# A retention-then-gated-linear-unit kernel: the first two units interleaved by hand, zero products in their waits, and gated jobs of one unit for the first four units

## The chip, the core and the metric

The kernel runs on one core of a Trainium2 chip. The metric is device time in microseconds (us) of one execution; lower is better. A profile of one execution shows the engines TensorE (PE; its weight loads are PEld), VectorE (DVE), ScalarE (ACT), GpSimd (POOL) and the queues that issue DMAs (SPq, ACTq).

## What is computed

```
scores = (1/sqrt(D)) * q @ k^T                        # per batch b and head h
ret    = (scores * gamma_h ** (i - j) for i >= j) @ v # decayed causal mask, no softmax
x      = ret, heads side by side                      # (8, 576, 512)
gate   = sigmoid(sum over k of conv_w[k] * x[t-4+k])  # causal convolution, 5 taps, per channel
out    = (gate * (x @ w_val)) @ w_out                 # (8, 576, 512), float32
```

The inputs are float32: q, k, v of shape (8, 8, 576, 64), w_val and w_out of (512, 512), conv_w of (5, 512). The decay is split into a factor on v (`gin`) and a factor on the output (`gout`).

## The kernel before

**Units and jobs.** The sequence of each of 8 batches is cut into two units of 256 positions and a rest of 64; the rests of four batches make one more unit. So there are 18 units, 0 to 17. Attention is done unit by unit, the gated part job by job: jobs 0 and 1 hold one unit each (256 columns), the others two units (512 columns).

**One unit's attention.** Three loads of 512 KB (`load`, L93, on SP's queue); `cast` (L201) of k, q and v to bf16, on GpSimd except k and q of unit 0; `turn` (L217): 16 transposes on TensorE into the PSUM pool `ps_a`; `take_turn` (L228): two copies out, `kq`; `scores` (L234): 16 products of quarter size for each half `hf` of the heads, into `ps_s`; `masks` (L248): VectorE multiplies by the mask, `p`; `update` (L325): products of k and v into `ps_s` (unit 0: `ps_v`), a ScalarE copy `xf`, and GpSimd sums that make the carried states; `carried` (L264): products of q with the carried states; `values` (L294): products with v; `take_x` (L306): VectorE scales the result into `xg`.

**The gated part.** `conv` (L387): the convolution as products with diagonal blocks `dg` into `ps_a`, then a sigmoid on ScalarE (`gate`); `value` (L405): `xg` times `wvb` into `ps_v`; `gated` (L415): VectorE multiplies both (`z`); `project` (L421): `z` times `wob` into `ps_v`, and a ScalarE copy `ob`; `store` (L431), on SP's queue. A job's conv and value are cut in two pieces over two steps where it has two units. The weights are made bf16 by `prep_wv` (ScalarE, L185) and `prep_wo` (VectorE, L190); `prep_conv` (L173) builds `dg`.

**Order.** The program is written out under a manual schedule: every engine takes its instructions in the order of the Python calls, and semaphores carry the waits between engines. The loop at L459 runs steps n = 0 to 20. Step n does scores and masks of unit n, conv and value of the piece that `PH` names, the values of unit n, cast of unit n+2, update and turn of unit n+1, and the projections that `PJ` names. `ps_a`, `ps_s` and `ps_o` hold one tile each, `ps_v` two; so conv waits until `take_turn` has emptied `ps_a`, scores of the second half until masks of the first has emptied `ps_s`, and a projection until a `gated` has emptied a `ps_v`. Loads run four units ahead (`ldp`, 4 buffers). Ahead of the loop stand eight products of zeros (`warm`, L193).

Of the kernel before, what the change touches and what calls it, by code (L numbers as in the profile page):

```python
# [21 lines left out]
def kernel(  # L22
# [32 lines left out]
    gp = ctx.enter_context(tc.tile_pool(name="gp", bufs=1))  # L55
# [15 lines left out]
    jobs = [(u,) for u in range(NC2)] + [(u, u + 1) for u in range(NC2, NU, 2)]  # L71
# [4 lines left out]
    with tc.manual_schedule():  # L76
# [24 lines left out]
        wof = consts.tile([P, NP, DM], F32, name="wof")  # L101
        nc.sync.dma_start(out=wvf, in_=moe_w_val.rearrange("(o i) n -> i o n", i=P))
        load(1)
# [3 lines left out]
        for u in range(2, 5):  # L107
            load(u)


        ident = consts.tile([P, P], BF16, name="ident")
# [5 lines left out]
        zero = consts.tile([P, 512], BF16, name="zero")  # L117
        nc.vector.memset(zero, 0.0)
# [41 lines left out]
        nc.vector.tensor_copy(mask[hi], mask_h[hi])  # L160
        mask_t = consts.tile([P, 2, P], BF16, name="maskt")
        nc.vector.tensor_copy(mask_t, mask)
        for i in (0, 2):
            nc.vector.memset(mask_t[i * 32:i * 32 + 32].rearrange("p j (r a) -> p j r a", r=2)[:, :, :, 32:64], 0.0)
# [7 lines left out]

        def prep_conv():  # L173
# [4 lines left out]
            id2 = consts.tile([P, 64], F32, name="id2")  # L178
            nc.vector.tensor_tensor(id2, ident[:, 0:64], ident[:, 64:128], op=ALU.add)
            nc.vector.tensor_tensor(  # L180
# [12 lines left out]
        def warm(n):  # L193
            z = ps_v.tile([P, 512], F32, name="v")
            for i in range(n):
                nc.tensor.matmul(z, lhsT=zero[:, 0:P], rhs=zero, start=True, stop=True)
# [3 lines left out]

        def cast(u):  # L201
            kind, b, c = units[u]
            kb = bfp.tile([P, 2, H, D], BF16, name="kb")
            qb = bfp.tile([P, 2, H, D], BF16, name="qb")
            vb = bfp.tile([P, H, 2, D], BF16, name="vb")
            ke, qe = (nc.vector.tensor_copy, nc.scalar.copy) if u == 0 else (nc.gpsimd.tensor_copy,) * 2
            ke(kb.rearrange("p r h d -> p h r d"), loaded["k", u].rearrange("p h (r d) -> p h r d", r=2))  # L207
            qe(qb.rearrange("p r h d -> p h r d"), loaded["q", u].rearrange("p h (r d) -> p h r d", r=2))  # L208
            nc.gpsimd.tensor_tensor(vb.rearrange("p h r d -> p (h r) d"),  # L209
# [249 lines left out]
        for n in range(NPH):  # L459
# [30 lines left out]
            if n == 1:  # L490
                prep_wo()
# [45 lines left out]
```

## Time and profile before

| | us |
|---|---|
| median of 3 runs | 176.27 (175.94 to 179.36) |
| the profiled execution | 176.73 |
| its span, first to last instruction | 175.0 |
| busy: PE, PEld | 148.3, 92.9 |
| busy: DVE, POOL, ACT | 99.4, 97.9, 89.0 |
| DMA read and written | 30.42 MB, 9.44 MB |

Times in the profile count from the first instruction of the span. A timeline line gives the start, how long a group of like instructions lasted, the engine, the line of the kernel, the operation, what it writes and reads, its form and how many there are; in brackets stand the idle time of the engine ahead of it and what ended it. A group of matrix products overlaps its neighbours in the record, since the end of a product is modelled: of the 0.42 us of 16 score products, some 0.35 us pass before the next group can start.

### The profile page before, as it was taken

Reading aid. Unit: us, or ns where it says so; the run is one execution under the profiler, and the core shown is the slowest. Engines: PE = TensorE matmul, PEld = TensorE weight load, DVE = VectorE, ACT = ScalarE, POOL = GpSimd, SP = SyncE. Lnnn points to the kernel's source line nnn. Section 1 sums busy time; section 2 is a strip of 40 time slices with the busy share of each in tenths; the row PEclk is TensorE's granted clock in tenths of the full one; section 3 lists DMA queues with packets and bytes.
Section 4 is the critical chain, followed back from the end, with each engine's and each line's share of the span. In section 5 each row is a group of like instructions: output and inputs, shape, how many; then the busy total and the mean of one; then the engine's idle time right before and its main releaser. Section 6 shows DMA issues by size and latency. Waiting matters only on the chain.

```text
span 175.0 us, 6597 instructions
## 1 busy us (share of the span) xinstructions
PE 148.3 (85%) x2921; PEld 92.9 (53%) x2921; DVE 99.4 (57%) x148; ACT 89.0 (51%) x118; POOL 97.9 (56%) x117
## 2 busy tenths in 40 slices
PE   5460767689596699999999999999999999999970
PEld 2150656576454465656666565666656566643320
DVE  5642232975636583765858376585838568583200
ACT  3547172527280538466373836647383653723550
POOL 7247369996692859495675949567594900000000
PEclk9999999999999999999999999999999999999999
DMA  4999999999996999999796998888611203032325
GB/s 143 358 351 291 285 269 321 290 329 322 316 339 195 301 342 302 295 265 321 227 301 234 306 299 257 241 277 243 204 54 73 120 4 124 2 124 120 122 62 180
DMA packets 60298, 40.28 MB, mean 230 GB/s; under 512 B 1626, under 2 KB 56942, under 8 KB 60270
## 3 DMA queue, kind: packets, MB, share of 16 engines
q1 hardware_dynamic: 60240, 39.85, 75.6%
q8 instruction: 23, 0.38, 0.8%
q14 instruction: 5, 0.04, 0.1%
q10 hardware_dynamic: 30, 0.01, 0.0%
HBM read 30.42 MB, written 9.44 MB: 228 GB/s over the span
## 4 chain that ended last, share of the span: by engine, by line
PE 61%; ACT 2%; DVE 1%; issue 0%; ACTq 0%
PE v L426 16%; PE v L410 14%; PE a L394 10%; PE a L224 7%; PE s L241 5%; PE o L302 4%; PE o L279 2%; PE s L339 1%; ACT gate L398 1%; DVE z L417 1%; PE o L286 1%; ACT ob L429 0%; ACTq L398 0%
## 5 line engine op out<-in xcount | busy, mean ns | idle before, releaser
L251 DVE TENSOR_TENSOR p<-s,mask 128x1024 bf16<-128x1024 f32 x32 | 39.2, 1224 | 44.5 <-PE s L241 44.5
L229 ACT COPY kq<-a 128x1024 bf16<-128x1024 bf16 x35 | 33.8, 1015 | 15.5 <-PE a L224 11.8
L209 POOL TENSOR_TENSOR vb<-fvc,gin 128x1024 bf16<-128x1024 f32 x18 | 34.5, 1917 | 5.3 <-DMA fvc<-in_v_dram 5.1
L410 PE MATMUL v<-xg,wvb 128*128 128x512 bf16 (+1 forms) x160 | 34.3, 359 | 0.0
L426 PE MATMUL v<-wob,z 128*128 128x512 bf16 x144 | 34.0, 379 | 0.1
L347 ACT COPY xf<-s 128x512 f32<-128x512 f32 x15 | 8.8, 585 | 42.5 <-PE s L339 42.5
L417 DVE TENSOR_TENSOR z<-gate,v 128x512 bf16<-128x512 f32 x36 | 24.5, 683 | 6.4 <-ACT gate L398 6.3
L241 PE MATMUL s<-kq 64*64 64x128 bf16 x576 | 19.8, 230 | 7.6 <-ACT kq L229 3.4
L394 PE MATMUL a<-xg,dg 64*64 64x512 bf16 (+1 forms) x400 | 24.1, 372 | 2.0 <-DVE xg L313 1.2
L398 ACT ACTIVATE gate<-a 128x1024 f32<-128x1024 f32 x18 | 18.4, 1024 | 11.9 <-ACT ob L429 5.8
L429 ACT COPY ob<-v 128x512 f32<-128x512 f32 x36 | 20.0, 606 | 8.2 <-PE v L426 8.2
L313 DVE TENSOR_TENSOR xg<-o,gout 128x512 bf16<-128x512 f32 x32 | 22.1, 744 | 2.0 <-PE o L302 2.0
L241 PEld LDWEIGHTS <-kq 64*64 64x64 bf16 x576 | 14.5, 109 | 15.2 <-issue 9.6
L410 PEld LDWEIGHTS <-wvb 128*128 128x128 bf16 x160 | 14.1, 97 | 14.0 <-issue 0.8
L426 PEld LDWEIGHTS <-z 128*128 128x128 bf16 x144 | 13.4, 98 | 14.1 <-issue 0.7
L207 POOL CAST kb<-fkc 128x1024 bf16<-128x1024 f32 x17 | 17.6, 1038 | 5.7 <-DMA fkc<-in_k_dram 5.7
L208 POOL CAST qb<-fqc 128x1024 bf16<-128x1024 f32 x17 | 17.7, 1040 | 0.9 <-DMA fqc<-in_q_dram 0.9
L394 PEld LDWEIGHTS <-dg 64*64 64x64 bf16 x400 | 13.6, 111 | 7.7 <-issue 2.8
L279 PE MATMUL o<-kq,s 64*64 64x128 bf16 x192 | 12.3, 220 | 5.8 <-POOL s L352 4.5
L224 PE MATMUL a<-ident,kb 128*128 128x128 bf16 x144 | 14.8, 230 | 2.5 <-DVE kb L207 2.5
L361 POOL TENSOR_TENSOR mid<-run,xf 128x256 f32<-128x256 f32 x8 | 5.8, 729 | 17.0 <-ACT xf L347 17.0
L279 PEld LDWEIGHTS <-s 64*64 64x64 bf16 x192 | 10.1, 108 | 8.8 <-POOL s L352 4.7
(60 smaller groups left out, 130.6 us busy)
## 6 DMA issues: line engine op xcount, KB each, us to landing
fkc<-in_k_dram SPq DMA_DIRECT2D x16, 512.0 KB, 6.0
fqc<-in_q_dram SPq DMA_DIRECT2D x16, 512.0 KB, 6.6
fvc<-in_v_dram SPq DMA_DIRECT2D x16, 512.0 KB, 7.3
out_dram<-ob SPq DMA_DIRECT2D x16, 512.0 KB, 3.4
wvf<-in_moe_w_val_dram SPq DMA_DIRECT2D x1, 1024.0 KB, 7.6
wof<-in_moe_w_out_dram SPq DMA_DIRECT2D x4, 256.0 KB, 7.2
fkc<-in_k_dram SPq DMA_DIRECT2D x8, 128.0 KB, 4.4
fqc<-in_q_dram SPq DMA_DIRECT2D x8, 128.0 KB, 4.4
```

The costliest lines, as they stand in the source:

```text
L209: nc.gpsimd.tensor_tensor(vb.rearrange("p h r d -> p (h r) d"), loaded["v", u].rearrange("p h (r d) -> p (h r) d", r=2), gin[:, c].rearran ...
L224: nc.tensor.transpose(ps[:, hf, i, prl, r, :], bf[u][i][:, r, h:h + 2, :].rearrange("p h d -> p (h d)"), ident)
L229: (eng or nc.scalar.copy)(kqt[u][hf].rearrange("p i l r c a -> p (i l r c a)"), tps[u][:, hf].rearrange("p i l r a -> p (i l r a)"))
L241: nc.tensor.matmul(s[half[c], par, prl, r, :], lhsT=t[half[par], 0, prl, r, c, :], rhs=t[half[par], 1, prl, :, c, :], start=True, stop=Tru ...
L251: nc.vector.tensor_tensor(p.rearrange("p e l r a -> p (e l) (r a)"), sps[u, hf].rearrange("p e l r a -> p (e l) (r a)"), m.rearrange("p r ...
L279: nc.tensor.matmul(o[rows, c, pr, :], lhsT=st[rows, pr, :], rhs=t[rows, 1, pr % 2, :, c, :], start=first(u, c, par), stop=False, skip_grou ...
L313: nc.vector.tensor_tensor(x[:, b, :, PAD + i0:PAD + i0 + P].rearrange("p o (a r) -> p o r a", r=2), o[:, c].rearrange("p o (r a) -> p o r ...
L394: nc.tensor.matmul(g[cols, bank, si, :], lhsT=dg[rows, blk, kk, :], rhs=xs(j, rows, blk, kk), start=(si == 0 and kk == 0), stop=(si == len ...
L398: nc.scalar.activation(t, g, AF.Sigmoid)
L410: nc.tensor.matmul(vp[:, si, :], lhsT=wvb[:, o, 2 * e + s, :], rhs=xs(j, slice(0, P), o, PAD), start=(si == 0 and o == 0), stop=(si == len ...
L417: nc.vector.tensor_tensor(zsb[j][:, 2 * e + ss[0]:2 * e + ss[-1] + 1, :], gsb[j, i][:, e], vps[j, i, e], op=ALU.mult)
L426: nc.tensor.matmul(o, lhsT=z[:, r, :], rhs=wob[:, jj, :], start=(jj == 0), stop=(jj == NP - 1))
```

## The change

It changes the first part of the program and the cut of the jobs:

- The loads of unit 1 are issued ahead of w_val instead of behind it; loads up to unit 6 are issued before the loop.
- The zero tile is VectorE's first instruction. `warm(8)` is replaced by `fill(n)`, called six times, 26 products in all, between other parts of the first two units.
- `dg` is built on GpSimd instead of VectorE. The casts of unit 0 are cut: k on VectorE, q half on ScalarE and half on VectorE; q of unit 1 is on ScalarE.
- `prep_mask_t` (for the tail units) is moved behind unit 1's attention.
- The attention of units 0 and 1 is written out by hand. The second scores of unit 0 go to `ps_a`; unit 0's values are done chunk by chunk; the second transposes of unit 1 are ahead of the rest of unit 0; `update` of units 0 and 1 uses `ps_v`; a dummy sigmoid loads ScalarE's table early.
- Then come, still ahead of the loop, conv, value and gated of jobs 0 and 1, with the w_out cast (`prep_wo`) on VectorE between the two jobs, projection of unit 0, turn of unit 2, projection of unit 1, update of unit 2, and the cast of unit 3.
- Jobs 0 to 3 have one unit each; from unit 4 on, jobs have two. The loop starts at n = 2. In step 2 there is no piece, in step 3 all of job 2, in steps 4 and 5 the two pieces of job 3; from step 6 on, the pieces fall on the same steps and the same units as before, and the projections too, except that units 2 and 3 are projected in steps 3 and 5 instead of 5 and 6.
- In a step, `carried(n, 1)` stands ahead of the second scores instead of among them, and `carried(n, 0)` between the two values calls instead of ahead of the second scores.
- The gate tile has two buffers instead of one, and in the last two steps the second half of a projection is copied by VectorE.

```diff
-    gp = ctx.enter_context(tc.tile_pool(name="gp", bufs=1))
+    gp = ctx.enter_context(tc.tile_pool(name="gp", bufs=2))
...
-    jobs = [(u,) for u in range(NC2)] + [(u, u + 1) for u in range(NC2, NU, 2)]
+    jobs = [(u,) for u in range(2 * NC2)] + [(u, u + 1) for u in range(2 * NC2, NU, 2)]
...
+        load(1)
         nc.sync.dma_start(out=wvf, in_=moe_w_val.rearrange("(o i) n -> i o n", i=P))
-        load(1)
...
-        for u in range(2, 5):
+        for u in range(2, 7):
...
+        zero = consts.tile([P, 512], BF16, name="zero")
+        nc.vector.memset(zero, 0.0)
...
-        zero = consts.tile([P, 512], BF16, name="zero")
-        nc.vector.memset(zero, 0.0)
...
-        nc.vector.tensor_copy(mask[hi], mask_h[hi])
         mask_t = consts.tile([P, 2, P], BF16, name="maskt")
-        nc.vector.tensor_copy(mask_t, mask)
-        for i in (0, 2):
-            nc.vector.memset(mask_t[i * 32:i * 32 + 32].rearrange("p j (r a) -> p j r a", r=2)[:, :, :, 32:64], 0.0)
+        def prep_mask():
+            nc.vector.tensor_copy(mask[hi], mask_h[hi])
+        def prep_mask_t():
+            nc.vector.tensor_copy(mask_t, mask)
+            for i in (0, 2):
+                nc.vector.memset(mask_t[i * 32:i * 32 + 32].rearrange("p j (r a) -> p j r a", r=2)[:, :, :, 32:64], 0.0)
...
+        id2 = consts.tile([P, 64], F32, name="id2")
+        nc.gpsimd.tensor_tensor(id2, ident[:, 0:64], ident[:, 64:128], op=ALU.add)
         def prep_conv():
             cps = ps_a.tile([P, KC * NP], F32, name="a")
             nc.tensor.transpose(cps, cwn, identf[0:KC * NP, 0:KC * NP])
             cw = consts.tile([P, KC * NP], F32, name="cw")
             nc.vector.tensor_copy(cw, cps)
-            id2 = consts.tile([P, 64], F32, name="id2")
-            nc.vector.tensor_tensor(id2, ident[:, 0:64], ident[:, 64:128], op=ALU.add)
-            nc.vector.tensor_tensor(
+            nc.gpsimd.tensor_tensor(
                 dg.rearrange("p o k j -> p k o j"),
                 cw.rearrange("p (k o) -> p k o", o=NP).unsqueeze(3).to_broadcast([P, KC, NP, 64]),
                 id2.unsqueeze(1).unsqueeze(1).to_broadcast([P, KC, NP, 64]), op=ALU.mult)
...
-        def warm(n):
+        def fill(n):
...
+        def cast1(u, n, eng=None, hs=slice(0, H)):
+            kind, b, c = units[u]
+            if (n, u) not in bf:
+                bf[n, u] = bfp.tile([P, H, 2, D] if n == "v" else [P, 2, H, D], BF16, name=f"{n}b")
+            t, src = bf[n, u], loaded[n, u]
+            if n == "v":
+                nc.gpsimd.tensor_tensor(t.rearrange("p h r d -> p (h r) d"), src.rearrange("p h (r d) -> p (h r) d", r=2),
+                                        gin[:, c].rearrange("p h r -> p (h r)").unsqueeze(2).to_broadcast([P, 2 * H, D]),
+                                        op=ALU.mult)
+            else:
+                (eng or nc.gpsimd.tensor_copy)(t[:, :, hs, :].rearrange("p r h d -> p h r d"),
+                                               src[:, hs].rearrange("p h (r d) -> p h r d", r=2))
         def cast(u):
-            kind, b, c = units[u]
-            kb = bfp.tile([P, 2, H, D], BF16, name="kb")
-            qb = bfp.tile([P, 2, H, D], BF16, name="qb")
-            vb = bfp.tile([P, H, 2, D], BF16, name="vb")
-            ke, qe = (nc.vector.tensor_copy, nc.scalar.copy) if u == 0 else (nc.gpsimd.tensor_copy,) * 2
-            ke(kb.rearrange("p r h d -> p h r d"), loaded["k", u].rearrange("p h (r d) -> p h r d", r=2))
-            qe(qb.rearrange("p r h d -> p h r d"), loaded["q", u].rearrange("p h (r d) -> p h r d", r=2))
-            nc.gpsimd.tensor_tensor(vb.rearrange("p h r d -> p (h r) d"),
-                                    loaded["v", u].rearrange("p h (r d) -> p (h r) d", r=2),
-                                    gin[:, c].rearrange("p h r -> p (h r)").unsqueeze(2).to_broadcast([P, 2 * H, D]),
-                                    op=ALU.mult)
-            bf[u] = (kb, qb, vb)
+            for n in "kqv":
+                cast1(u, n)
...
+        def turn1(u, hf, i):
+            if u not in tps:
+                tps[u] = ps_a.tile([P, 2, 2, 2, 2, P], BF16, name="a")
+                kqt[u] = [tp_sb.tile([P, 2, 2, 2, 2, 64], BF16, name=f"kq{x}") for x in range(2)]
+            for prl in range(2):
+                for r in range(2):
+                    h = 2 * (2 * hf + prl)
+                    nc.tensor.transpose(tps[u][:, hf, i, prl, r, :],
+                                        bf["kq"[i], u][:, r, h:h + 2, :].rearrange("p h d -> p (h d)"), ident)
+        def turn(u):
+            for hf in range(2):
+                for i in range(2):
+                    turn1(u, hf, i)
...
-        def scores(u, hf, between=None):
-            s = ps_s.tile([P, 2, 2, 2, P], F32, name="s")
+        def scores(u, hf, pool=None):
+            s = (pool or ps_s).tile([P, 2, 2, 2, P], F32, name="a" if pool else "s")
...
-                    if between and prl == 0 and r == 0:
-                        between()
...
-        def fence(u, rows):
-            t = consts.tile([P, 1], F32, name="fence", bufs=2)
-            nc.vector.tensor_copy(t[rows], ops[u][rows, 1, 0, 0:1])
-        def values(u, hf):
-            vb = bf[u][2]
+        def fence(u):
+            t = consts.tile([P, 1], F32, name="fence")
+            nc.vector.tensor_copy(t[lo], ops[u][lo, 1, 0, 0:1])
+        def values(u, hf, chunks=(0, 1)):
+            vb = bf["v", u]
+            if u not in ops:
+                ops[u] = ps_o.tile([P, 2, NP, P], F32, name="o")
             o = ops[u]
             p = pt[u, hf]
             for prl in range(2):
                 pr = 2 * hf + prl
                 for r in range(2):
                     for (c, par) in QUAD:
-                        nc.tensor.matmul(o[half[par], c, pr, :], lhsT=vb[half[c], 2 * pr + par, r, :],
-                                         rhs=p[half[c], par, prl, r, :], start=first(u, c, par),
-                                         stop=(r == 1), skip_group_check=True)
-        def take_x(u):
+                        if c in chunks:
+                            nc.tensor.matmul(o[half[par], c, pr, :], lhsT=vb[half[c], 2 * pr + par, r, :],
+                                             rhs=p[half[c], par, prl, r, :], start=first(u, c, par),
+                                             stop=(r == 1), skip_group_check=True)
...
+        def take_x(u, chunks=(0, 1)):
...
+            for c in chunks:
...
-        def update(u):
+        def update(u, early=False):
...
-            if u == 0:
+            kb, vb = bf["k", u], bf["v", u]
...
-        def sets(j, i):
-            return (0, 1) if len(jobs[j]) == 1 else (i,)
-        def conv(j, i):
-            n, ss = width(j), sets(j, i)
-            g = ps_a.tile([P, 2, len(ss), n], F32, name="a")
+        gps = {}
+        def conv(j, ss, take=True):
+            n = width(j)
+            gt = ps_a.tile([P, 2, 512], F32, name="a")
+            g = gt[:, :, 0:len(ss) * n].rearrange("p e (s t) -> p e s t", s=len(ss))
...
+            gps[j, ss] = g
+            if take:
+                take_gate(j, ss)
+        def take_gate(j, ss):
+            n = width(j)
             t = gp.tile([P, 2, len(ss), n], F32, name="gate")
-            nc.scalar.activation(t, g, AF.Sigmoid)
-            gsb[j, i] = t
-            if i == 0:
+            nc.scalar.activation(t, gps[j, ss], AF.Sigmoid)
+            gsb[j, ss] = t
+            if j not in zsb:
...
-        PH = {1: [(0, 0)], 2: [(1, 0)], 3: []}
-        PJ = {2: [(0, 0)], 3: [(1, 0)]}
-        for j in range(NC2, len(jobs)):
-            n = 2 * j
-            PH[n], PH[n + 1] = [(j, 0)], [(j, 1)]
-            PJ[n + 1] = [(j, 0)]
-            PJ[n + 2] = [(j, 1)]
-        NPH = 2 * len(jobs) + 1
-        warm(8)
+        vcopy, scopy = nc.vector.tensor_copy, nc.scalar.copy
+        h0, h1 = slice(0, 4), slice(4, 8)
+        def value_all(j, ss, e):
+            value(j, ss, e)
+            gated(j, ss, e)
+        def proj(j, m, eng=None):
+            for r in range(2):
+                project(j, m, r, eng if r else None)
+            store(jobs[j][m])
+        fill(10)
+        prep_gout((0, 1))
+        cast1(0, "k", vcopy)
+        prep_mask()
         prep_conv()
-        prep_gout((0, 1))
-        cast(0)
-        turn(0, ((0, 0), (1, 0), (0, 1), (1, 1)))
-        take_turn(0, 0, nc.vector.tensor_copy)
+        turn1(0, 0, 0)
+        turn1(0, 1, 0)
+        fill(4)
+        cast1(0, "q", scopy, h0)
+        cast1(0, "q", vcopy, h1)
+        prep_gout((2,))
+        turn1(0, 0, 1)
+        turn1(0, 1, 1)
+        take_turn(0, 0, vcopy)
         take_turn(0, 1)
-        for n in range(NPH):
+        prep_gout((3,))
+        fill(2)
+        cast1(0, "v")
+        scores(0, 0)
+        masks(0, 0)
+        scores(0, 1, ps_a)
+        masks(0, 1)
+        dummy = consts.tile([P, 1], F32, name="dummy")
+        nc.scalar.activation(dummy, lsc, AF.Sigmoid)
+        cast1(1, "k")
+        fill(5)
+        update(0, True)
+        cast1(1, "q", scopy)
+        values(0, 0, (0,))
+        values(0, 1, (0,))
+        take_x(0, (0,))
+        turn1(1, 0, 0)
+        turn1(1, 1, 0)
+        carried(0, 1)
+        fence(0)
+        turn1(1, 0, 1)
+        turn1(1, 1, 1)
+        cast1(1, "v")
+        values(0, 0, (1,))
+        carried(0, 0)
+        values(0, 1, (1,))
+        take_turn(1, 0, vcopy)
+        take_turn(1, 1)
+        take_x(0, (1,))
+        fill(3)
+        scores(1, 0)
+        masks(1, 0)
+        conv(0, (0, 1), False)
+        update(1, True)
+        take_gate(0, (0, 1))
+        carried(1, 1)
+        scores(1, 1)
+        masks(1, 1)
+        prep_wv()
+        fill(2)
+        values(1, 1)
+        carried(1, 0)
+        values(1, 0)
+        take_x(1)
+        prep_mask_t()
+        cast(2)
+        value_all(0, (0, 1), 0)
+        conv(1, (0, 1))
+        value_all(0, (0, 1), 1)
+        prep_wo()
+        value_all(1, (0, 1), 0)
+        value_all(1, (0, 1), 1)
+        proj(0, 0)
+        turn(2)
+        take_turn(2, 0)
+        take_turn(2, 1)
+        proj(1, 0)
+        update(2)
+        cast(3)
+        PH = {3: (2, (0, 1)), 4: (3, (0,)), 5: (3, (1,))}
+        PJ = {3: [(2, 0)], 5: [(3, 0)]}
+        for j in range(2 * NC2, len(jobs)):
+            n = 2 * j - 2
+            PH[n], PH[n + 1] = (j, (0,)), (j, (1,))
+            PJ.setdefault(n + 1, []).append((j, 0))
+            PJ.setdefault(n + 2, []).append((j, 1))
+        NPH = 2 * len(jobs) - 1
+        for n in range(2, NPH):
             att = n < NU
             if n + 5 < NU:
                 load(n + 5)
-            piece = PH.get(n, [])
+            piece = PH.get(n)
             if att:
                 scores(n, 0)
                 masks(n, 0)
-            if n == 0:
-                cast(1)
-                update(0)
-                prep_gout((2, 3))
-            for (j, i) in piece:
-                conv(j, i)
+            if piece:
+                conv(*piece)
             if att:
-                if n == 0:
-                    scores(n, 1)
-                    masks(n, 1)
-                    carried(n, 0)
-                    fence(0, hi)
-                    carried(n, 1)
-                    fence(0, lo)
-                    prep_wv()
-                else:
-                    carried(n, 0)
-                    scores(n, 1, lambda: carried(n, 1))
-                    masks(n, 1)
-            for (j, i) in piece:
+                carried(n, 1)
+                scores(n, 1)
+                masks(n, 1)
+            if piece:
                 for e in range(2):
-                    value(j, i, e)
-                    gated(j, i, e)
-            if n == 1:
-                prep_wo()
+                    value_all(*piece, e)
             if att:
                 values(n, 1)
+                carried(n, 0)
                 values(n, 0)
                 take_x(n)
             if n + 2 < NU:
...
                 take_turn(n + 1, 0)
                 take_turn(n + 1, 1)
             for (j, m) in PJ.get(n, []):
-                project(j, m, 0)
-                project(j, m, 1)
-                store(jobs[j][m])
+                proj(j, m, vcopy if n >= NPH - 2 else None)
```

## The prediction

> **What bounds the kernel now.** I read the page's slices first, then the busy time by stage, then the chain that ended last, and last the timeline of the first 75 us.
>
> ```profile
> PE   5460767689596699999999999999999999999970
> ...
> DMA  4999999999996999999796998888611203032325
> ```
>
> ```profile
> 20.00:25.00 5.00, 3.69 (x95) 3.21 (x88) 1.54 (x3) 2.50 (x3) 2.08 (x2) 1.00 0.98 280
> ...
> 50.00:60.00 10.00, 6.91 (x169) 4.51 (x172) 5.58 (x7) 5.00 (x7) 5.93 (x7) 1.00 0.89 260
> ...
> 70.00:100.00 30.00, 30.00 (x638) 18.72 (x636) 19.64 (x24) 17.43 (x24) 21.16 (x25) 1.00 0.93 276
> ```
>
> ```profile
> 75.24 1.22 PE a L394 x20
> ...
> 77.20 1.83 PE v L410 x8
> 79.03 0.57 PE o L302 x32
> 79.60 0.25 PE s L339 x32
> 79.86 1.00 PE a L224 x16
> 80.86 1.73 PE v L426 x8
> 82.58 0.35 PE s L241 x16
> 82.93 1.22 PE a L394 x20
> ```
>
> A slice is 4.4 us, and the columns after the window's length are PE, PEld, DVE, ACT and POOL. From 60 us on TensorE never stops, and the chain repeats one step each 7.69 us (82.93 - 75.24), all of it TensorE's own work: conv 1.2, value 1.8, projection 1.7, attention 3.0. So what the change can win lies ahead of 60 us, where waits between engines rule, and it is kept only as far as the steady part starts earlier.
>
> ```profile
> 1.90 3.60 PE L196 MATMUL v<-zero 128*128 128x512 bf16 x8 [1.90 <-DVE tok L123]
> ...
> 25.06 2.35 PE L394 MATMUL a<-xg,dg 64*64 64x256 bf16 x40 [0.27 <-ACT kq L229]
> ...
> 31.33 1.90 POOL L209 TENSOR_TENSOR vb<-fvc,gin 128x1024 bf16<-128x1024 f32 x1 [0.22 <-PE v L410]
> ...
> 31.87 2.45 DVE L191 CAST wob<-wof 128x2048 bf16<-128x2048 f32 x1
> ...
> 33.09 1.93 ACT L229 COPY kq<-a 128x1024 bf16<-128x1024 bf16 x2 [0.31 <-PE a L224]
> ...
> 34.15 0.42 PE L241 MATMUL s<-kq 64*64 64x128 bf16 x16 [1.10 <-ACT kq L229]
> ...
> 35.76 1.29 PE L394 MATMUL a<-xg,dg 64*64 64x256 bf16 x40 [1.19 <-DVE xg L313]
> ...
> 42.86 0.42 PE L241 MATMUL s<-kq 64*64 64x128 bf16 x16
> 43.05 1.09 ACT L429 COPY ob<-v 128x512 f32<-128x512 f32 x2
> ...
> 53.86 0.30 PE L241 MATMUL s<-kq 64*64 64x128 bf16 x7 [1.44 <-issue]
> ...
> 75.18 1.27 PE L394 MATMUL a<-xg,dg 64*64 64x512 bf16 x20
> ```
>
> The scores of units 2 and 3 start at 34.15 and 42.86. The 75.18 row is the conv of step 7: up to it both kernels have done the same units, pieces and projections, and behind it they do the same work. I therefore follow the new order to that conv and compare.
>
> The same 40 products took 2.35 us at 25 us and 1.29 at 36, so TensorE ran at half speed early, though the granted clock reads 1.00 in each window. Each zero product took some 0.43 us.
>
> **The change, step by step.** I take every engine's new order, in turn, with the durations of the rows.
>
> Start, up to unit 0's scores. The zero tile is ready at about 1.1 (VectorE waited until 1.40 for the identity), ten zero products at 0.43 end at 5.5. k of unit 0 is cast at once on its landing (0.69, done 5.5, before at 8.2). The small transpose and copy for `dg` free `ps_a` at 6.1. The q cast waits for its load (6.14) and ends at 6.7. With TensorE at full speed: k transposes 0.6, four zeros 0.86, q transposes 0.6, to 8.1; VectorE's copy 0.69, then ScalarE's 1.01, to 9.9; first mask 9.35 to 10.55, second to 11.8. At half speed these products take 1.03 + 1.7 + 1.06, and all is 1.8 later.
>
> `dg` on GpSimd is not in the trace. GpSimd's rows give 1.9 ns per column (vb) to 2.8 ns (L361, 0.73 us for 256), so 1280 columns cost 2.4 to 3.6; I take 2.4, the row with a like broadcast. It ends at 8.5, vb of unit 0 at 10.5; the longer end would add up to 0.5. It saves VectorE 1.7 us ahead of the k cast.
>
> Units 0 and 1. The load of unit 1 passes w_val (1024 KB, about 3 us), so its waits at 12.37, 13.84 and 15.73 become about 9.3, 10.8 and 12.5; w_val lands near 15.7, and unit 2 stays at 22.4 to 25.4, the bytes ahead of it being the same. After ScalarE's gout 0.8 and table load 1.28 (to 12.15), xf 0.65 to 12.8 and q of unit 1 1.04 to 13.9. GpSimd: s, run, s 1.5 to 14.0, vb 1.9 to 15.95. TensorE transposes q of unit 1 to 14.5, finishes unit 0's values at 15.0; copies of kq to 15.2 and 16.2; scores of unit 1 at 15.6 (before 24.15), conv of job 0 16.25 to 17.45 (before 25.06). Then xf, gate, w_val cast 0.65 + 1.02 + 2.16, to 21.7; the state of unit 1 at 19.35, its second scores to 20.05, mask to 21.3, values with carried 0.9, take_x 1.38 to 23.6. Here the new kernel is 8 us ahead of the old one.
>
> Where the lead goes. VectorE's queue then holds: the tail mask (0.5, to 24.1), gated, gated, the w_out cast, gated, gated. Conv of job 1 must wait for take_x and ends at 24.85, the second value product at 25.75, its gated at 26.5, the w_out cast 2.45 at 28.95, the next gated at 29.65. Only that frees a `ps_v` for the first projection, 29.7 to 31.5, and behind it in TensorE's queue stand the transposes of unit 2, though its casts are done at 27.3. They end at 32.5. ScalarE then has kq 1.93, ob 1.09, xf 0.58, to 36.15, and the scores of unit 2 wait for that xf to empty `ps_s`: 36.2, against 34.15 before. GpSimd idles from 27.3 to 36.15, since the cast of unit 3 is queued behind the state of unit 2 that needs this xf: 1.5 + 3.9, to 41.55. Update 0.35, transposes 1.0, kq 1.0: scores of unit 3 at 43.95, against 42.86.
>
> Steps 3 to 6. In step 3 GpSimd's next cast (3.9) and the state (1.15) hold the carried products to 46.6; then scores 0.65, value 1.85, values 0.85, update and turn 1.25, projection 1.75: unit 4 at 53.0. Step 4 has no projection, and its two masks are 1.22 each with little between: values at 56.3 to 57.05, turn to 58.3, kq 1.0: unit 5 at 59.35. Step 5: the second kq to 60.3, conv, carried and scores to 61.45, mask 1.23 to 62.7, values 0.8, turn 1.25, projection 1.75: unit 6 at 66.5 (before 67.15). Step 6 without projection is 5.95 and then shows kq's 1.93: conv of step 7 at 74.4, against 75.18. The sum is -0.7 us.
>
> Cut of jobs 2 and 3: 40 convs of 256 columns took 1.1 to 1.3, 20 of 512 took 1.2; 16 value products 1.85 against 1.83. I take 0. Order in a step: 8 carried products alone took 0.2 to 0.3, among the scores some 0.2, so 0 to 0.1 for each of 12 steps; and the second scores wait for the mask anyway (68.85 to 68.90). I take 0, and keep +1.2 for the range. The VectorE copy at the end replaces 0.58 on ScalarE; nearest are 0.69 and 0.75: -0.1 to +0.2, I take 0. The second gate buffer takes no wait away, since the last gated is long done. SP's queue: the loads of unit 7 now stand behind two stores, as DMA writes of 512 KB each some 3 us together; unit 7 landed by 54 and is cast after 57, so this is hidden; without the cover it would cost those 3 us.
>
> The stall of 1.44 us at 53.86, which no engine's wait explains, is in the old span alone in my sum; a like one is worth 0 to 1.9. I add 0.4, since most of the new waits would hide it.
>
> [...]
>
> Total: 176.73 - 0.7 + 0.4 = 176.4 by the profiled run; the median of the runs is 0.46 lower. I say 176.0.
>
> **Rivals.** (1) The lead of 8 us at job 0 is largely kept. For it: TensorE has only some 27.5 us of work between 36 and 74 (five attentions of 3.0, three convs with values of 3.0, two projections of 1.7), so 10 us of slack is there to win, and the queue waits are summed by hand. Against: in-order queues, the w_out cast ahead of gated, the GpSimd chain. Without the 2.45 cast in the way, and with half of unit 3's wait (2 us) gone: 171.5.
>
> (2) TensorE stays at half speed through unit 1, as it did up to 25 us before. Then the fills themselves cost: 1.8 at the first scores, 1.1 more for the five zeros and 0.6 for three, 1.1 in the conv, and 1.0 in transposes and scores: 5.6 later at conv of job 0, all of which the chain behind carries on: 181.5. If speed comes with the five zeros, only 2.0 is lost: 178. It decides if half speed lasts past some 14 us. For it: eight zeros did not suffice before. Against: ten, and more right behind.
>
> (3) The order does what it says and nothing is won: this is my forecast, lead given back.
>
> **How the numbers follow.** A difference under 2% (3.5 us) can hardly be told here from none. Forecast with full speed early 0.45 and with speed by the five zeros 0.18, both within 2%; rival 1 0.2; rival 2 0.17. So faster 0.2, same 0.63, slower 0.17. The likeliest case alone runs from 174.5 (no stall, -1 from shorter waits) to 178.5 (carried order +1.2, stall 1.9). The range takes in most of both rivals: 171.5 to 181.0.
>
> **What would show it.** Right: scores of unit 1 near 16, conv of job 0 near 17 at 1.2 us, the w_out cast right ahead of the first projection, scores of unit 2 near 36, GpSimd idle for 8 us before them, conv of step 7 near 74. Wrong: scores of unit 2 before 33 (rival 1), or conv of job 0 at 2.3 us and later than 20 (rival 2), or a steady step off 7.69 us.

## The result, and the profile after

The changed kernel takes 185.22 us (median of 4 runs, 183.07 to 186.86), against 176.47 (175.94 to 179.36) for the kernel before, run beside it: 1.0423 times as long, interval 1.0319 to 1.0528. The prediction said 176.0 and a range to 181.0. The profiled run took 184.44, with a span of 182.5. Some executions of a kernel last 1.5% or more beyond its shortest one, so ratios, intervals and differences between kernels below go by the mean of the others (183.76 for the change, 176.29 for the kernel before).

The slices of the changed kernel's page, 4.56 us each:

```profile
PE   7878369854699869969999999999999999999980
PEclk9999957997569999987999999999999999999997
DMA  4999999999996699599388989879822023022216
```

TensorE starts at once, as planned, and from about 84 us on it never stops (in the kernel before, from 60 on). New is the second line: the granted clock dips three times, at about 23, 43 and 81 us. The share by stage of the changed kernel (length, then PE, PEld, DVE, ACT, POOL busy, granted clock, DMA share, GB/s):

```profile
20.00:30.00 10.00, 6.88 (x114) 4.67 (x115) 4.73 (x7) 3.11 (x6) 5.72 (x6) 0.66 1.05 310
40.00:50.00 10.00, 5.77 (x139) 4.67 (x132) 4.44 (x5) 2.51 (x3) 9.87 (x11) 0.67 1.05 332
80.00:90.00 10.00, 9.50 (x180) 5.83 (x181) 5.13 (x6) 4.25 (x5) 6.37 (x8) 0.83 0.78 225
90.00:120.00 30.00, 30.00 (x638) 18.91 (x627) 20.46 (x24) 17.27 (x25) 21.11 (x24) 1.00 0.87 256
```

The trace's clock records place the spells: full from 5.84, half for 6.83 us from 22.91, half for 10.24 from 43.39, half for 3.41 from 80.94, full from 84.35 to 179.93. That is 20.5 us at half speed behind the first release. The last window is the steady part, and it is like the one before the change.

The chain of the changed kernel that ended last, at the first convs (start, length):

```profile
80.92 2.35 PE a L408 x19
...
90.20 1.27 PE a L408 x20
...
91.95 1.83 PE v L430 x8
...
97.90 1.27 PE a L408 x20
```

The convs are those of steps 7, 8 and 9. The steady step is 97.90 - 90.20 = 7.70 us, as before, and the conv of step 8 stands at 90.20 where it stood at 82.93: 7.27 of the profiled runs' 7.71 us are lost ahead of it. The timeline of the changed kernel up to there (start, length, engine, line, in brackets the idle time ahead and what ended it):

```profile
15.84 0.42 PE L254 MATMUL s<-kq 64*64 64x128 bf16 x16
...
16.20 1.29 PE L408 MATMUL a<-xg,dg 64*64 64x256 bf16 x40
...
19.03 0.41 PE L353 MATMUL v<-vb,kb 64*64 64x64 bf16 x26 [1.48 <-issue]
...
25.95 1.32 DVE L166 COPY maskt<-mask 128x256 bf16<-128x256 bf16 x1
...
27.68 2.27 PE L408 MATMUL a<-xg,dg 64*64 64x256 bf16 x40
...
31.57 1.22 DVE L196 CAST wob<-wof 128x2048 bf16<-128x2048 f32 x1
...
39.70 0.42 PE L254 MATMUL s<-kq 64*64 64x128 bf16 x16 [1.38 <-ACT xf L361]
39.72 0.40 POOL L366 CAST s<-xf 128x256 bf16<-128x256 f32 x1 [12.53 <-ACT xf L361]
...
48.71 0.64 PE L254 MATMUL s<-kq 64*64 64x128 bf16 x16 [1.10 <-ACT kq L242]
49.62 2.35 PE L408 MATMUL a<-xg,dg 64*64 64x256 bf16 x40 [0.27 <-ACT kq L242]
...
80.92 2.35 PE L408 MATMUL a<-xg,dg 64*64 64x512 bf16 x20 [0.49 <-ACT kq L242]
```

Unit 1's scores (15.84) and the conv of job 0 (16.20) stand where they were predicted (15.6, 16.25). From there the kernel falls behind its forecast. The 40 products of a conv take 1.29 us at 16.20, but 2.27 and 2.35 at 27.68 and 49.62: these two lie in the half-speed spells.

### The profile page after: what moved, and what is told of

Same layout as the page of the kernel before. It is cut to its first block, busy times and chain, and to the rows that moved or that the text cites. A ratio compares the mean times of both kernels' runs of the same rounds, so it can differ in the third digit from the quotient of the medians.

```text
span 182.5 us, 6766 instructions
## 1 busy us (share of the span) xinstructions
PE 158.3 (87%) x2995; PEld 99.5 (55%) x2995; DVE 101.7 (56%) x151; ACT 87.7 (48%) x119; POOL 98.5 (54%) x118
## 4 chain that ended last, share of the span: by engine, by line
PE 51%; DVE 1%; ACT 1%; issue 0%; ACTq 0%
PE v L445 14%; PE v L430 11%; PE a L408 10%; PE a L233 5%; PE o L317 4%; PE s L254 4%; PE o L290 2%; PE s L353 1%; ACT gate L418 1%; DVE z L436 1%; PE o L297 1%; DVE ob L448 0%; ACTq L418 0%
## 5 line engine op out<-in xcount | busy, mean ns | idle before, releaser
L430 PE MATMUL v<-xg,wvb 128*128 128x512 bf16 (+1 forms) x176 | 36.1, 352 | 1.1 <-DVE xg L327 1.1
L436 DVE TENSOR_TENSOR z<-gate,v 128x512 bf16<-128x512 f32 (+1 forms) x38 | 24.7, 656 | 9.5 <-ACT gate L418 6.3
L418 ACT ACTIVATE gate<-a 128x1024 f32<-128x1024 f32 (+1 forms) x19 | 18.7, 983 | 19.0 <-PE a L408 8.3
L408 PE MATMUL a<-xg,dg 64*64 64x512 bf16 (+1 forms) x440 | 26.4, 377 | 1.3 <-ACT kq L242 1.3
L430 PEld LDWEIGHTS <-wvb 128*128 128x128 bf16 x176 | 16.1, 101 | 15.5 <-issue 3.3
L254 PE MATMUL s<-kq 64*64 64x128 bf16 x560 | 16.0, 229 | 6.5 <-ACT kq L242 3.4
L317 PE MATMUL o<-p,vb 64*64 64x128 bf16 x576 | 17.2, 229 | 2.8 <-DVE p L262 2.8
L254 PEld LDWEIGHTS <-kq 64*64 64x64 bf16 x576 | 11.7, 109 | 14.2 <-issue 8.5
L317 PEld LDWEIGHTS <-vb 64*64 64x64 bf16 x576 | 13.5, 109 | 9.1 <-issue 9.0
L366 POOL CAST s<-xf 128x256 bf16<-128x256 f32 x8 | 3.2, 398 | 26.3 <-ACT xf L361 25.5
```

The costliest lines, as they stand in the source:

```text
L254: nc.tensor.matmul(s[half[c], par, prl, r, :], lhsT=t[half[par], 0, prl, r, c, :], rhs=t[half[par], 1, prl, :, c, :], start=True, stop=Tru ...
L317: nc.tensor.matmul(o[half[par], c, pr, :], lhsT=vb[half[c], 2 * pr + par, r, :], rhs=p[half[c], par, prl, r, :], start=first(u, c, par), s ...
L408: nc.tensor.matmul(g[cols, bank, si, :], lhsT=dg[rows, blk, kk, :], rhs=xs(j, rows, blk, kk), start=(si == 0 and kk == 0), stop=(si == len ...
L418: nc.scalar.activation(t, gps[j, ss], AF.Sigmoid)
L430: nc.tensor.matmul(vp[:, si, :], lhsT=wvb[:, o, 2 * e + s, :], rhs=xs(j, slice(0, P), o, PAD), start=(si == 0 and o == 0), stop=(si == len ...
L436: nc.vector.tensor_tensor(zsb[j][:, 2 * e + ss[0]:2 * e + ss[-1] + 1, :], gsb[j, ss][:, e], vps[j, ss, e], op=ALU.mult)
```

## The experiments

Theory 1: the clock. Waits leave TensorE so idle that the clock falls back, above all in steps 2, 4 and 6, out of which gated work was moved. Rival A: the queues. Unit 2's update and turn stand behind the w_out cast and the projections. Rival B: the cut of the jobs. Theory 2, formed on the way: a step of attention lasts nearly as long whether gated work fills its waits or not, so gated work done ahead of the loop costs its full time.

In the table, the third column is the mean of the executions that differences go by, and the conv of step 7 is that of the profiled execution.

| kernel | median (range), us | mean, us | profiled, us | ratio to before [interval] | conv of step 7 |
|---|---|---|---|---|---|
| the kernel before | 176.47 (175.94-179.36) | 176.29 | 176.73 | 1 | 75.18 |
| the change | 185.22 (183.07-186.86) | 183.76 | 184.44 | 1.0423 [1.0319, 1.0528] | 80.92 |
| e1_hold | 179.66 (178.33-181.32) | 179.22 | 178.33 | 1.0253 [1.006, 1.0446] | 76.33 |
| e2_ten_only | 185.11 (183.09-185.14) | 184.61 | 185.1 | 1.0561 [1.0422, 1.0701] | 83.17 |
| e3_turn_first | 180.62 (179.55-181.93) | 180.68 | 179.55 | 1.0358 [1.0204, 1.0512] | 77.47 |
| e4_before_jobs | 177.7 (176.2-179.29) | 177.2 | 177.3 | 1.0137 [0.9977, 1.0297] | 75.79 |
| e5_hold_turn | 178.4 (176.91-180.74) | 178.15 | 176.91 | 1.0106 [1.0048, 1.0164] | 75.08 |
| e6_before_fills | 177.0 (174.33-178.72) | 175.58 | 178.72 | 0.9984 [0.9931, 1.0037] | 77.08 |
| e7_value_first | 178.09 (177.22-179.12) | 178.08 | 177.22 | 1.0111 [1.0065, 1.0158] | 75.25 |
| e8_hold_late | 182.81 (181.44-184.97) | 182.36 | 181.44 | 1.0344 [1.0277, 1.0412] | 79.29 |
| e10_pieces_in | 175.46 (172.37-177.6) | 173.34 | 174.41 | 0.9829 [0.9746, 0.9911] | 72.46 |
| e9_pieces_hold | 172.21 (171.15-172.91) | 172.13 | 171.82 | 0.9764 [0.9701, 0.9827] | 69.92 |

Each ratio is to executions of the kernel before that were run beside that kernel; their means went from 175.08 to 176.35 us, so differences of 1 us between rows say little by themselves.

### e1_hold: the change with its clock held

The change, with 52 more products of zeros in the waits of TensorE (the places that the expectation lists add up to 52, not to its 43); nothing is reordered.

```diff
+        fill(7, ps_s, "s")          # ahead of carried(1, 1)
-        fill(2)
+        fill(6)                     # behind prep_wv()
+        fill(6, ps_a, "a")          # ahead of value_all(0, (0, 1), 0)
+        fill(7, ps_o, "o")          # behind cast(3)
+                if n == 2: fill(5, ps_a, "a")      # ahead of scores(n, 1), again behind masks(n, 1)
+                if n == 2: fill(3, ps_a, "a")      # ahead of update
+                if n in (2, 4, 6): fill(5, ps_s, "s")  # behind turn(n + 1)
```

> The changed kernel with 43 more zero products in the places where its TensorE waits between 19 and 80 us (7 before the carried products of unit 1, 4 more after the w_val cast, 6 before the first value products, 7 before step 2, 13 in step 2, 5 behind the transposes of steps 2, 4 and 6), in PSUM tiles that nobody uses there; the order of all else is kept. Theory 1 (the clock that falls back to half speed at 22.9, 43.4 and 80.9 us is what the forecast missed): full speed is held from about 6 us on, conv of step 7 comes near 75 to 77 instead of 80.9, and the time falls by some 6 us to 177 to 179.5. Theory 2 (the queues: w_out cast, projections and ScalarE copies ahead of unit 2; the clock falls only where TensorE waits for others anyway and costs little by itself): full speed is held and the time stays above 183. Theory 3 (the stall of 1.5 us at 17.5 us that no engine explains): it is still there, worth 1.5 us.

The clock is full from 6.42 to 173.67 without a break, and 4.5 of the 7.5 us lost are back (183.76 - 179.22 of 183.76 - 176.29). The windows of e1_hold and its convs of steps 7 and 8:

```profile
20.00:30.00 10.00, 10.00 (x151) 6.44 (x150) 6.49 (x9) 4.24 (x7) 5.79 (x6) 1.00 1.07 313
40.00:50.00 10.00, 9.08 (x192) 6.33 (x191) 5.20 (x6) 3.54 (x4) 9.94 (x11) 1.00 1.06 325
```

```profile
76.33 1.28 PE L408 MATMUL a<-xg,dg 64*64 64x512 bf16 x20 [0.49 <-ACT kq L242]
...
84.01 1.27 PE L408 MATMUL a<-xg,dg 64*64 64x512 bf16 x20
```

The conv of step 8 comes 6.2 us earlier than in the change, with more work on TensorE. Theory 1 holds for the larger part of the loss: 60% by the times, 6.2 of 7.3 us by these two profiles. The rest has another cause, since e1_hold is still slower than before.

### e8_hold_late: which spell costs what

e1_hold without its added fills in unit 1 and ahead of job 0's values (the one right ahead of step 2 stays).

```diff
-        fill(7, ps_s, "s")
-        fill(6)
+        fill(2)
-        fill(6, ps_a, "a")
```

> The changed kernel with the extra zero products of step 2 and later alone (none of those ahead of 27 us). Theory 1 by spells: the clock falls back near 23 us as in the changed kernel and comes back near 30, and isn't lost again at 43 and 81; conv of step 7 near 78, total 180.5 to 182.5, that is about two thirds of the gain of holding it throughout.

Only the first spell comes back (half from 23.04 to 29.86). So the first spell is worth about 3.1 us (182.36 - 179.22), and the two later ones 1.4 by the times (183.76 - 182.36) or 3.2 by the conv of step 8 (90.20 against 86.97), not the two thirds that were expected.

### e2_ten_only and e6_before_fills: what the release is worth

e2_ten_only is the change without its 16 later fills. e6_before_fills is the kernel before, with an early zero tile and fills in the waits of its first units.

```diff
-        fill(4)        # e2: and fill(2), fill(5), fill(3), fill(2)
```

```diff
-        warm(8)                  # e6
+        warm(10)
+        warm(6)                  # behind prep_conv()
+        warm(4, ps_o, "o")       # behind take_turn(0, 1), and behind update(0)
+        warm(12, ps_o, "o")      # behind the second masks of unit 0
+        warm(5)                  # behind turn(1), and behind conv in step 1
```

> The changed kernel without the zero products behind the first ten (4, 2, 5, 3 and 2 of them left out). Theory 1: the clock is released near 6 us or not, and falls back within 7 us; scores of unit 1 some 1 to 2 us later, conv of job 0 at 2.3 us, total 185 to 188. Theory 2: the 16 products left out only took TensorE's idle time, the total stays within 1 us of 184.5.

> The kernel before with zero products in its first waits and nothing else moved (10 instead of 8 ahead, 6 behind the small transpose, 4 behind the transposes of unit 0, 4 behind its update, 12 behind its second scores, 5 behind the transposes of unit 1, 5 behind the conv of job 0; the zero tile is VectorE's first instruction). If half speed up to 27.8 us costs the kernel before something: full speed from about 6 us, scores of unit 1 at 22 to 23 instead of 24.15, conv of job 0 at 1.3 instead of 2.35 us, total 173 to 175. If the first 28 us wait for other engines and loads alone: 176 to 177.

In e2_ten_only the clock came at 4.98, was gone at 8.40, and was at half speed for 30.7 us in three spells up to 56.18. The scores of unit 1 came 1.2 us later, and still the total is nearly the same: 184.61 against 183.76. The change's own 16 later fills, which hold the clock to 22.9, win less than 1 us. In e6_before_fills the clock came at 5.24 instead of 27.76, fell at 18.89 and at 59.85, and nothing was won (0.9984, interval 0.9931 to 1.0037). Its scores of unit 1 came at 26.45, not at the 22 to 23 that were expected, and its total is the one that was expected if the first 28 us wait for other engines and loads alone. So an early release that wasn't held won little in either order; what one held throughout would win in the old order wasn't tried.

### e3_turn_first and e5_hold_turn: the queues

Unit 2 goes ahead of the w_out cast and job 1, in the change (e3) and in e1_hold (e5).

```diff
         value_all(0, (0, 1), 1)
+        update(2)
+        turn(2)
+        take_turn(2, 0)
+        take_turn(2, 1)
+        cast(3)
         prep_wo()
         value_all(1, (0, 1), 0)
         value_all(1, (0, 1), 1)
         proj(0, 0)
-        turn(2)
...
         proj(1, 0)
```

> The changed kernel with update, transposes and copies of unit 2 and the cast of unit 3 moved ahead of the w_out cast, of job 1's value products and of both projections. Theory 2: scores of unit 2 come some 3 to 5 us earlier than 39.7 (behind the projections, but with their copies done and the state of unit 2 not behind ScalarE's copies), GpSimd's wait of 12.5 us shrinks to 5 or less, cast of unit 3 ends by 40, total 178 to 181. Theory 1 alone: the order gains only what the clock lets it, the clock still falls back in step 2 and 6, total 182 or more.

> Both edits at once: the extra zero products that held the clock, and unit 2's update, transposes and copies and unit 3's cast ahead of the w_out cast and the projections. Theory 2 (the order behind unit 1 itself gives the lead away): with the clock held, moving unit 2 ahead still brings conv of step 7 from 76.3 to 72 to 74, total 175 to 177.5. Theory 1 alone (moving unit 2 ahead only helped because TensorE was kept busier and the clock fell back less): 179 to 180, as with the clock held and the old order.

In e3 the total fell into the range expected for the queues, but not on that way: unit 2's scores came at 40.43, not 3 to 5 us earlier, and the 3.1 us were won behind them, with one spell at half speed (22.48 to 32.72) instead of three. With the clock held, the same move is worth 1.1 us by the times (179.22 to 178.15) and 1.3 by the conv of step 7, where 72 to 74 was expected. Rival A in this form falls as the main cause. Job 1's values and both projections still stand ahead of unit 2's scores in TensorE's queue in both; that part of the queues is theory 2's.

### e7_value_first and e4_before_jobs: two small suspects

e7 is e5_hold_turn with both value products of job 0 ahead of `take_x(1)`, without the six fills that stood before them, with job 0's `gated` ahead of job 1's conv and the tail mask at the end. In the change, the first value product waited 1.15 us for unit 1's `take_x`, which writes the same tile but other data. e4 is the kernel before with the change's cut of the jobs alone.

```diff
+        value(0, (0, 1), 0)         # e7
+        value(0, (0, 1), 1)
         take_x(1)
```

```diff
-    jobs = [(u,) for u in range(NC2)] + [(u, u + 1) for u in range(NC2, NU, 2)]     # e4
+    jobs = [(u,) for u in range(2 * NC2)] + [(u, u + 1) for u in range(2 * NC2, NU, 2)]
```

> The kernel with both edits, and in it the value products of job 0 issued ahead of unit 1's take_x instead of behind it (the first of them waits for take_x, which writes other columns of the same tile), their gated ahead of the conv of job 1, and the tail mask made behind the projections. If that wait is on the path: 1 to 2 us less than with both edits, conv of step 7 at 71 to 73. If the w_out cast or GpSimd's queue ends last there anyway: the same within 0.5 us.

> The kernel before with one part of the change alone: jobs 2 and 3 hold one unit each, with their conv and value in steps 3 and 4 and their projections in steps 4 and 5 (so step 5 has no piece and step 6 no projection); all else as before. If the cut of the jobs costs or wins nothing: within 1 us of the kernel before. Theory 1 adds: if the clock falls back behind step 6, where no projection follows the transposes, 1.5 to 2 us more.

Neither matters much: 178.08 against 178.15 for e7, so that wait isn't on the path. e4's 1.0137 has an interval from 0.9977 to 1.0297, too wide by itself. Its profile says more: the steps with the new cut, from unit 3's scores to those of step 7, take 31.36 us (43.52 to 74.88) against 31.96 before (42.86 to 74.82, with the stall of 1.44 in it), and no clock is lost. So the cut costs at most some 1 us. Rival B falls.

### e10_pieces_in and e9_pieces_hold: the gated work back in the steps

e10 is the change without a fill added: unit 2's update and turn follow job 0's values at once, job 1 goes into step 2, and the projections of units 0 to 3 into steps 2, 3, 4 and 6. It also has job 0's values ahead of `take_x(1)`, as in e7, and the w_out cast and the tail mask behind unit 3's cast. e9 is the same with 29 more zero products.

```diff
-        PH = {3: (2, (0, 1)), 4: (3, (0,)), 5: (3, (1,))}
-        PJ = {3: [(2, 0)], 5: [(3, 0)]}
+        PH = {2: (1, (0, 1)), 3: (2, (0, 1)), 4: (3, (0,)), 5: (3, (1,))}
+        PJ = {2: [(0, 0)], 3: [(1, 0)], 4: [(2, 0)], 6: [(3, 0)]}
```

```diff
+        fill(7, ps_s, "s")      # e9: ahead of carried(1, 1)
+        fill(6)                 # for fill(2)
+        fill(8, ps_a, "a")      # ahead of update(2)
+        fill(5, ps_s, "s")      # behind take_turn(2, 1), and behind turn in step 5
```

> The same with zero products in the waits left (7 ahead of unit 1's carried products, 6 behind the w_val cast, 8 ahead of unit 2's update, 5 behind its transposes, 5 behind those of step 5). Theory 1 and theory 2 together: full speed from 6 us on, scores of unit 2 near 31, conv of step 7 near 70 to 72, total 171 to 174, below the kernel before. Theory 1 alone (order does not matter once the clock is held): 178 to 179.5.

> The changed kernel with job 1's conv, value products and both first projections put back into steps: update, transposes and copies of unit 2 right behind the value products of job 0, conv and value of job 1 in step 2, projections of units 0 to 3 in steps 2, 3, 4 and 6; no zero product added. Theory 2, sharpened (a step's attention is a chain of waits of 6.5 to 7.6 us whether or not gated work fills it, so gated work done ahead of the loop gives its time away): scores of unit 2 near 33 instead of 39.7, conv of step 7 near 73 to 75, total 176 to 179, and fewer half-speed spells since the waits are filled. If half speed alone costs: the first spell near 23 us stays and the total is above 181.

Both beat the kernel before, and e9_pieces_hold is the fastest of all: 172.21, beside 176.35 for the kernel before there, ratio 0.9764 (0.9701 to 0.9827). Step 2 of e9_pieces_hold, then steps 2 and 3 of e5_hold_turn, from score to score:

```profile
31.24 0.42 PE L254 MATMUL s<-kq 64*64 64x128 bf16 x16
32.12 1.29 PE L408 MATMUL a<-xg,dg 64*64 64x256 bf16 x40 [0.46 <-ACT kq L242]
33.75 1.92 PE L430 MATMUL v<-xg,wvb 128*128 128x256 bf16 x16
...
37.55 1.89 PE L445 MATMUL v<-wob,z 128*128 128x512 bf16 x7
39.37 0.42 PE L254 MATMUL s<-kq 64*64 64x128 bf16 x16
```

```profile
36.54 0.42 PE L254 MATMUL s<-kq 64*64 64x128 bf16 x16
...
44.16 0.42 PE L254 MATMUL s<-kq 64*64 64x128 bf16 x16
```

With a conv, its values and a projection in it (some 5 us of TensorE), step 2 lasts 8.13 us; with fills alone in their place, 7.62. But fills can lengthen a step too: 7.62 there, against 6.70 for attention alone in the first window below. Three windows without a fill in them, at the full clock, settle what the work costs: step 2 of e3_turn_first, which holds attention alone, then step 3 of the kernel before and of e4_before_jobs, which differ by the conv and values of one job:

```profile
40.43:47.13 6.70, 3.16 (x121) 2.69 (x120) 3.83 (x4) 2.23 (x4) 5.50 (x7) 1.00 1.09 354
```

```profile
42.86:50.12 7.26, 4.84 (x137) 3.39 (x136) 3.84 (x4) 3.43 (x6) 5.63 (x8) 1.00 1.08 324
```

```profile
43.52:51.23 7.71, 7.71 (x193) 6.00 (x192) 5.02 (x6) 4.51 (x7) 5.64 (x8) 1.00 1.09 330
```

Attention alone keeps TensorE busy for 3.16 of 6.70 us. A conv with values, 3 us, lengthens a step by 0.45 (7.26 to 7.71); all 5 us by some 1.4 (6.70 to 8.13, between kernels that differ in more). Ahead of the loop they were paid in full: unit 2's scores start at 36.54 in e5 and at 31.24 in e9, and the 5.3 us between them are still there at the conv of step 7 (75.08, 69.92), 5.16 of them. Theory 2 holds, with "nearly free" for free. In e10 the same step lasts 9.89, with the w_out cast at its head.

Order old or new, without added fills and with them: 183.76 and 179.22; 173.34 and 172.13. So the order is worth 10.4 us, or 7.1 with the clock held. The clock is worth 4.5 in the old order and 1.2 in the new one, where without added fills it was lost for two spells of 3.41 us only. The two pairs don't have the same fills, and they ran on different chips, so these are sizes and not a clean split.

## Why the prediction was wrong, point by point

**The step that failed** is "With TensorE at full speed", said at the start and carried unspoken through unit 1 and steps 2 to 6. Rival 2 asked only whether the release would come late, and it came at 5.84, early enough; that it could be lost again is in no term of the sum. That the fills would bring full speed in time was the author's estimate, shown by no row of the kernel before, where 40 products still took 2.35 us at 25.06 behind eight of them; the runs showed the clock come at 5.84 in the change and go at 22.91, and come at 4.98 in e2_ten_only and go at 8.40. The chain was right but for that: in e1_hold, where the clock holds, it is met to 0.5 us at unit 1 and to 1.1 to 1.9 behind it.

| start, us | predicted | the change | e1_hold |
|---|---|---|---|
| scores of unit 1 | 15.6 | 15.84 | 16.06 |
| scores of unit 2 | 36.2 | 39.70 | 37.65 |
| scores of unit 3 | 43.95 | 48.71 | 45.50 |
| scores of unit 4 | 53.0 | 58.79 | 54.08 |
| scores of unit 5 | 59.35 | 65.55 | 60.84 |
| scores of unit 6 | 66.5 | 72.81 | 68.23 |
| conv of step 7 | 74.4 | 80.92 | 76.33 |
| conv of step 8 | 82.1 | 90.20 | 84.01 |

The predicted conv of step 8 is that of step 7 and one steady step, 74.4 + 7.69. Of the 8.1 us missed there, 6.2 are the clock's (90.20 to 84.01). The other 1.9 stand in e1_hold too, and 1.4 of them are the stall named below.

**The idle stretches ahead of two of the three falls stood in the prediction's own numbers.** It had the second scores of unit 1 and two zeros, and little else, between the conv of job 0 (end 17.45) and the second mask (end 21.3). And it had an attention's 3.0 us of TensorE alone in step 2, from 36.2 to 43.95. The three windows ahead of the three losses in the changed kernel, each as long as its shortest spell at half speed, 3.41 us:

```profile
19.50:22.91 3.41, 1.17 (x25) 0.69 (x26) 1.05 (x1) 3.41 (x7) 2.44 (x4) 1.00 1.07 312
39.98:43.39 3.41, 1.17 (x46) 0.77 (x37) 2.45 (x2) 0.00 (x0) 3.35 (x6) 1.00 1.14 328
77.53:80.94 3.41, 1.76 (x66) 1.42 (x58) 1.85 (x4) 2.51 (x3) 2.19 (x4) 1.00 1.05 300
```

TensorE is busy for 34, 34 and 52% of them. In the kernel before, in such windows from the first clock record at 27.76 on, the idlest up to 165 us is this one, 58%, and the clock stays full:

```profile
51.64:55.05 3.41, 1.97 (x33) 1.23 (x29) 1.02 (x2) 1.02 (x1) 2.01 (x2) 1.00 0.78 228
```

Two of the falls lie in steps that lost gated work, 2 and 6; in step 4, which lost some too, the clock held. The first, worth 3.1 us (e8), lies in unit 1, ahead of the loop, where TensorE waits 1.70 us for GpSimd's state and 0.80 for a mask. The prediction saw the granted clock as full or half at the start of the program, not as something that goes again later, as it did at 22.91, 43.39 and 80.94.

**The lead given back in queues**: the lead was given back, but the place of unit 2's update and turn in the queues was a small part of it (1.1 to 1.3 us, e5 against e1). GpSimd idled before unit 2's state from 27.2 to 39.72, near the predicted 27.3 to 36.15. The reason is theory 2: gated work that lay in waits before was put where it lay in no wait.

**Single terms.** The w_out cast took 1.22 us, not 2.45; the tail mask's copy 1.32, where 0.5 stood for the whole mask; `dg` on GpSimd 2.57, not 2.4. The wait of job 0's value product for unit 1's `take_x`, 1.15 us, wasn't foreseen, and e7 shows that it costs nothing. The cut of the jobs and the tail, both set at 0, came near it (at most some 1 us in e4; 7.71 - 7.27 = 0.44 behind step 8). The stall was set at 0.4 and came in full, 1.48 at 19.03.

## What to carry to other kernels

Work that filled the waits of a step bound by latency was cheap here (0.45 of 3 us and 1.4 of 5 us); moved ahead of the loop, it cost its full time, however early it got done (5.16 us at the conv of step 7, e5_hold_turn against e9_pieces_hold). Where TensorE waits much, add up its busy time along the forecast chain, and read the clock records of the first profile beside it: here the clock went behind windows of 3.41 us with 34, 34 and 52% of it, and 52 products of zeros in the waits held it and won 4.5 us (e1_hold). An early release of the clock that was lost again won next to nothing (0.9984 in e6_before_fills; 0.85 us between e2_ten_only and the change).

## What the runs showed of the hardware

**How long the spells were, and how busy TensorE was ahead of them.** Behind the first release, the half-speed spells lasted 6.83, 10.24 and 3.41 us in the change, 6.82 in e8_hold_late, 10.24 in e3_turn_first and twice 3.41 in e10_pieces_in. In windows of 3.413 us from 5.84 to 165 us of the change, those at whose end the clock fell had TensorE busy for 34, 34 and 52%; the least busy that kept it had 52% (63.87 to 67.28), 56% (16.08 to 19.49) and 60% (36.56 to 39.97). At half speed, windows with 60, 82 and 60% did not end the spell (22.91, 43.39 and 46.80), and the three that ended one had 100% (26.32, 50.21 and 80.93). So two windows with the same 52% went different ways, and this case has no single share at which the clock falls. In e1_hold, the stretches 19.50 to 22.91 and 39.98 to 43.39 had TensorE busy for 100 and 93%, fills included, at the full clock.

**The clock before its first record reads as full.** In the kernel before, the record begins at 27.76 us; ahead of that the windows show a granted clock of 1.00 while the same 40 products took 2.35 us instead of 1.29.

**In three kernels, where a VectorE cast or copy and a GpSimd operation overlapped by much, the later one took longer.** The w_out cast took 2.45 us when it started behind a GpSimd operation in the kernel before (at 31.87, behind 31.33), and 1.22 in the change, where GpSimd was idle. The tail mask's copy took 1.32 us in the change, behind a GpSimd operation that had started at 25.29, and 0.21 in e5_hold_turn, where none had started ahead of it. In e10_pieces_in the cast comes first:

```profile
30.41 1.27 DVE L196 CAST wob<-wof 128x2048 bf16<-128x2048 f32 x1
30.54 2.04 POOL L216 CAST kb<-fkc 128x1024 bf16<-128x1024 f32 x1
```

The w_out cast keeps its time, and the k cast behind it takes 2.04 us, 1.04 elsewhere.

**A stall that no semaphore explains.** TensorE stood still among unit 1's update products (`v`, L353 in the change) for 1.48 us up to 19.03 in the change, and there in seven of the eight kernels made from it, for 1.2 (e7_value_first) to 2.7 us (e3_turn_first); e2_ten_only has none. In the kernel before it stood still for 1.44 up to 53.86. Shorter ones stand in e6_before_fills (1.00 at 57.85), e5_hold_turn (0.49 at 61.12) and e8_hold_late (0.57 at 65.74). By the record all that it needed was in place each time. What holds it there, no run shows.
